# A fourth product by inner products in the first layer of the last sequence, and a new order of that layer

## The chip, the cores and the metric

The kernel runs on one NeuronCore of a Trainium2 chip. The metric is the device time of one execution in microseconds, the median over several runs. TensorE (PE in the rows, its weight loads PEld) multiplies matrices into PSUM, VectorE (DVE), ScalarE (ACT) and GpSimd (POOL) work on elements, and SyncE (SP) issues most of the DMAs. Each engine takes its instructions from a queue of its own; semaphores tie them together.

## The reference

Four sequences of 768 rows go through clustered attention (not touched here) and then through a normalised two-layer network:

```python
mu = np.mean(x, axis=-1, keepdims=True)
var = np.mean((x - mu) ** 2, axis=-1, keepdims=True)
xn = (x - mu) / np.sqrt(var + 1e-06) * g_ln
ch = np.maximum(xn @ w_ch1, 0.0) @ w_ch2     # 768x512 @ 512x2048, then 768x2048 @ 2048x512
return (x + ch)
```

All of it is float32. The change lies in `xn @ w_ch1` of the last sequence.

## The kernel before

Each layer is a matrix product done by Winograd's form of Strassen's method: the operands are cut in two by two blocks, and seven block products with sums before and after them take the place of eight. The block products are numbered 1 to 7 as in the code.

**The outer products.** In the first layer the 2048 columns are 16 chunks of 128; chunks j and j+8 (j = 0 to 7) make one unit. `first_layer(b, j, part)` does outer product `part` of unit j: two chunks of 128 of the inner dimension times 384 columns of x, into one PSUM bank. Products 1, 6, 7 and 4 add up in the same bank `st["x"]`, so each must wait until ScalarE has copied the bank's state so far (`kept`, line 930): after 1 comes p1, after 6 u2, after 7 u3; after 4 the bank is taken out by ScalarE with a ReLU (line 972).

**The inner products.** From sequence 2 on (`paired_layer`), two units (a pair, g = 0 to 3) share some outer products, which are split once more: `inner_products` makes an outer product of a pair out of seven products of one chunk of 128 times 192 columns. The code calls the outer product that is made so by a letter: "A" is product 2, "B" is 5, "C" is 3. The seven inner products come in four steps: step 1 makes inner products 1 and 2, step 2 makes 6 and 5, step 3 makes 7, step 4 makes 4 and 3. Below, "c2" is step 2 of C for the pair before, "A1" step 1 of A for the pair at hand. In each letter the inner products 1, 6, 7 and 4 again add up in one bank: the next of them may start only when the state after the one before has been taken out. For A and C VectorE does that, with an addition (line 1372; in the rows `pi<-x_ps,p` for A and `a<-x_ps,lower` or `pi<-x_ps,lower` for C), for B a copy by ScalarE (line 1374, `kept<-x_ps`). A further VectorE addition (line 1378) finishes each output. PSUM has six banks for the `x` and `z` tiles of all these products.

**Other VectorE work in the layer.** `onto_first(j, l)` (line 1567, 128x768) adds B's result to the u2 and u3 of a pair; C adds onto what it leaves. `outer_sums` (lines 1184, 1186, 1188, 128x768 each) makes the operands of the second layer out of a finished pair. `inner_x` (line 1330, four instructions of 128x192) makes the operands of a letter out of x. `unit_end` takes some jobs of the sequence before from a list (`pending`): an addition (line 1292, `m<-m,rest_x`, 128x768) and a transpose (line 1298, `y<-m`).

**What sets the order.** The order is written out by hand: `OUTER` lists the outer products of a pair slot by slot, and `inner_plan` says which inner steps stand behind each slot. Within a slot an engine's queue gets first the outer product, then what `onto_first` adds, then the inner steps, `inner_x`, the ReLUs (`relu`, line 943), `outer_sums`, the weight loads (`w_load`), and the jobs of `unit_end`. `manual_schedule` keeps this order on TensorE, VectorE, ScalarE and SyncE. The second layer (`deep_layer`, lines 1236 and 1251) follows; its weights come through a ring of ten slots in `w2`, filled by `ring_load`.

The lines that say when a bank may be used again are these, in `inner_products`:

```python
            nc.tensor.matmul(
                bank, p["w"][way], p["x"][way], start=way in (1, 2, 5), stop=True, skip_group_check=True
            )
            if way in add:
                ...
                if p["onto"]:
                    nc.vector.tensor_tensor(o, bank, p["onto"](*at), ALU.add)
                else:
                    nc.scalar.copy(o, bank)
```

Of the kernel before, what the change touches and what calls it, by code (L numbers as in the profile page):

```python
# [23 lines left out]
def kernel(  # L24
# [1297 lines left out]
    w1_d = {n: spill.tile([NPU, P, 4 * P], F32, name=f"w1_d{n}") for n in (2, 5, 3)}  # L1322
# [27 lines left out]
    def w1_pair(j):  # L1350
        return [[w1_block(0, 1, j + i)[:, k] for k in range(2)] for i in range(2)]
# [31 lines left out]
    def flat(t):  # L1383
        return t.rearrange("p a c -> p (a c)")
# [47 lines left out]
    def w_load(b, n, g):  # L1432
# [17 lines left out]
        if b == LAST and n:  # L1450
            nc.sync.dma_start(out=w_in[5][:, 512:] if n == 5 else w_in[n], in_=w1_d[n][g])
# [8 lines left out]
    def inner_plan(g, last):  # L1460

        if not last:
# [17 lines left out]
        plan = {  # L1480
            1: [("C", g - 1, 4), ("B", g, 3)], 2: [("B", g, 4), ("A", g, 1)], 3: [("A", g, 2)],
            4: [("A", g, 3)], 5: [("A", g, 4)], 6: [("C", g, 1)],
            7: [("C", g, 2), ("B", g + 1, 1)], 8: [("C", g, 3), ("B", g + 1, 2)],
        }
        if g == 0:
            plan |= {
                1: [], 2: [("B", g, 1)], 3: [("B", g, 2), ("A", g, 1)], 4: [("A", g, 2), ("B", g, 3)],
                5: [("B", g, 4), ("A", g, 3)], 6: [("A", g, 4), ("C", g, 1)],
            }
        elif g == NPU - 1:  # L1490
            plan |= {5: [("A", g, 4), ("C", g, 1)], 6: [("C", g, 2)], 7: [("C", g, 3)], 8: [("C", g, 4)]}
        return plan

    def paired_layer(b):
# [734 lines left out]
```

## Time and profile before

| | |
|---|---|
| median of 3 runs | 866.61 us (866.16 to 867.55) |
| the profiled execution | 866.26 us, of which the span from first to last instruction is 864.7 us |
| TensorE busy | 859.5 us (99% of the span) |
| VectorE busy | 741.4 us (86%) |
| ScalarE busy | 426.8 us (49%) |
| the chain that ended last | TensorE 97% |
| last sequence's first layer | 729.36 to 796.75 us from the span's start |

The profiled execution lies 0.35 us under the median. Busy time of TensorE is counted from modelled ends, and its instructions overlap, so its spacing is read from the starts.

### The profile page before, as it was taken

Reading aid. Unit: us, or ns where it says so; the run is one execution under the profiler, and the core shown is the slowest. Engines: PE = TensorE matmul, PEld = TensorE weight load, DVE = VectorE, ACT = ScalarE, POOL = GpSimd, SP = SyncE. Lnnn points to the kernel's source line nnn. Section 1 sums busy time; section 2 is a strip of 40 time slices with the busy share of each in tenths; the row PEclk is TensorE's granted clock in tenths of the full one; section 3 lists DMA queues with packets and bytes.
Section 4 is the critical chain, followed back from the end, with each engine's and each line's share of the span. In section 5 each row is a group of like instructions: output and inputs, shape, how many; then the busy total and the mean of one; then the engine's idle time right before and its main releaser. Section 6 shows DMA issues by size and latency. Waiting matters only on the chain.

```text
span 864.7 us, 13888 instructions
## 1 busy us (share of the span) xinstructions
PE 859.5 (99%) x4818; PEld 598.7 (69%) x4818; DVE 741.4 (86%) x1304; ACT 426.8 (49%) x809; POOL 143.5 (17%) x231
## 2 busy tenths in 40 slices
PE   8999999999999999999999999999999999999998
PEld 5444444444444446668887667998778999777998
DVE  6999999999999979888967898898887897776876
ACT  6877789888888836551003543111664110444110
POOL 2012121222222213220000210002440002250000
PEclk9999999999999999999999999999999999999999
DMA  8777889999976538978695688875556975455776
GB/s 165 140 131 132 155 170 188 204 210 207 190 166 179 136 131 234 280 189 313 206 272 151 224 275 247 285 202 176 155 150 207 347 204 178 125 152 171 255 205 139
DMA packets 229354, 169.63 MB, mean 196 GB/s; under 512 B 159056, under 2 KB 180032, under 8 KB 228256
## 3 DMA queue, kind: packets, MB, share of 16 engines
q1 hardware_dynamic: 192768, 139.44, 58.8%
q0 software_dynamic: 11776, 24.79, 13.2%
q10 hardware_dynamic: 24736, 4.48, 2.8%
q8 instruction: 39, 0.64, 0.3%
q14 instruction: 35, 0.29, 0.1%
HBM read 119.67 MB, written 40.59 MB: 185 GB/s over the span
## 4 chain that ended last, share of the span: by engine, by line
PE 97%; DMA 1%; DVE 1%; SPq 0%; ACT 0%; issue 0%; DVEq 0%; ACTq 0%
PE x_ps L901 19%; PE s_ps L426 18%; PE a_ps L438 15%; PE x_ps L1236 12%; PE z_ps L1236 6%; PE x_ps L1018 5%; PE z_ps L901 5%; PE x_ps L1363 5%; PE y_ps L1236 3%; PE z_ps L1018 2%; PE z_ps L1363 2%; PE sim_ps L334 2%; PE den_ps L504 1%; PE y_ps L1018 1%; PE y_ps L1363 1%; DMA out_dram<-y 1%
## 5 line engine op out<-in xcount | busy, mean ns | idle before, releaser
L426 PE MATMUL s_ps<-t,t 64*128 64x384 f32 x768 | 154.7, 483 | 0.0
L1312 POOL DMA_DIRECT2D out_dram<-y x66 | 51.1, 782 | 268.2 <-DVE y L1298 187.9
L426 PEld LDWEIGHTS s_ps<-t,t 64*128 64x128 f32 x768 | 68.0, 187 | 39.1 <-issue 38.1
L1236 PE MATMUL x_ps<-lower,w 128*128 128x192 f32 x448 | 80.5, 326 | 0.0
L1236 PEld LDWEIGHTS x_ps<-lower,w 128*128 128x128 f32 x448 | 74.2, 190 | 0.8
L418 ACT ACTIVATE e<-s_ps 128x768 f32<-128x768 f32 x83 | 66.7, 813 | 3.1 <-PE s_ps L426 2.6
L418 ACT ACTIVATE w<-s_ps 128x768 f32<-128x768 f32 x80 | 64.5, 813 | 4.1 <-PE s_ps L426 3.6
L426 PE MATMUL s_ps<-mask,mask 64*128 64x384 bf16 x384 | 62.7, 323 | 0.3 <-ACT e L418 0.2
L943 ACT ACTIVATE lower<-lower 128x384 f32<-128x384 f32 x88 | 42.9, 520 | 35.5 <-DVE lower L935 30.4
L930 ACT COPY p<-x_ps 128x384 f32<-128x384 f32 x31 | 14.7, 475 | 92.5 <-PE x_ps L901 85.6
L438 PE MATMUL a_ps<-e,v_sb 128*64 128x384 f32 x336 | 57.6, 488 | 0.0
L438 PE MATMUL a_ps<-w,v_sb 128*64 128x384 f32 x320 | 55.2, 488 | 0.0
L303 POOL DMA_DIRECT2D w<-tb x32 | 29.2, 912 | 153.7 <-DVE tb L300 139.9
L901 PE MATMUL x_ps<-xn,w 128*128 128x384 f32 x128 | 46.6, 487 | 0.0
L901 PE MATMUL x_ps<-xn,ws 128*128 128x384 f32 x128 | 46.6, 487 | 0.0
L901 PE MATMUL x_ps<-xt,w 128*128 128x384 f32 x128 | 46.5, 486 | 0.0
L901 PE MATMUL x_ps<-xt,ws 128*128 128x384 f32 x128 | 46.3, 486 | 0.0
L438 PEld LDWEIGHTS a_ps<-e,v_sb 128*64 128x64 f32 x336 | 23.5, 137 | 30.9 <-issue 28.6
L438 PEld LDWEIGHTS a_ps<-w,v_sb 128*64 128x64 f32 x320 | 22.4, 137 | 30.0 <-issue 28.4
L426 PEld LDWEIGHTS <-mask 64*128 64x128 bf16 x384 | 19.0, 94 | 34.3 <-issue 10.4
L1249 ACT COPY u<-x_ps 128x192 f32<-128x192 f32 x30 | 9.6, 319 | 65.9 <-PE x_ps L1236 61.3
L380 ACT ACTIVATE mask<-oh,far 32x384 bf16<-32x384 bf16 x61 | 37.3, 612 | 3.2 <-DVE oh L363 1.9
(347 smaller groups left out, 1894.8 us busy)
## 6 DMA issues: line engine op xcount, KB each, us to landing
w<-w_d SPq DMA_DIRECT2D x84, 256.0 KB, 3.4
raw<-in_moe_w_ch_dram SPq DMA_DIRECT2D x32, 512.0 KB, 4.9
w<-w_t SPq DMA_DIRECT2D x36, 256.0 KB, 5.1
w<-tb POOLq DMA_DIRECT2D x32, 256.0 KB, 5.9
w<-w_all SPq DMA_DIRECT2D x27, 256.0 KB, 3.3
v_sb<-in_v_dram SPq DMA_DIRECT2D x32, 192.0 KB, 3.9
xr<-x_d SPq DMA_DIRECT2D x24, 256.0 KB, 3.5
q_sb<-in_q_dram SPq DMA_DIRECT2D x62, 96.0 KB, 3.9
```

The source lines that it names most:

```text
L303: nc.gpsimd.dma_start(out=w, in_=fb, accum_op=ALU.add)
L334: nc.tensor.matmul(sim[r : r + Q, :HC], cT[:, pr, :, :].rearrange("p j c -> p (j c)"), prepared[n][side][:, g * HC : (g + 1) * HC], start= ...
L380: nc.scalar.activation(out, oh[src, :], AF.Identity, bias=add, scale=factor)
L418: nc.scalar.activation(e, st["both", i][:, :, :HC], AF.Exp, scale=SCALE)
L426: nc.tensor.matmul(banks[j][:, :HC], of_keys[:, keys], of_queries[:, o : o + HC], start=part == first, stop=part != first, skip_group_chec ...
L438: nc.tensor.matmul(acc[j * D : (j + 1) * D, :HC], loaded[n]["v"][:, j, c, :], e[:, j, :], start=(c == 0), stop=(c == NT - 1),)
L901: nc.tensor.matmul(bank[:, :HC], lhs[:, c, :], rhs[:, c], start=first and c == 0, stop=c == NDH - 1, skip_group_check=True,)
L943: nc.scalar.activation(h, h, AF.Relu)
L1018: nc.tensor.matmul(bank[:, :MH].rearrange("p (h f) -> p h f", h=2), hidden[lhs + (c,)][:, tt * P : (tt + 1) * P], rhs[:, :, c], start=firs ...
L1236: nc.tensor.matmul(bank, w[:, c, :], a[:, c], start=(way in (1, 2, 5) or alone) and c == 0, stop=c == NQH - 1, skip_group_check=True,)
L1312: queues[i % len(queues)].dma_start(out=to, in_=y)
L1363: nc.tensor.matmul(bank, p["w"][way], p["x"][way], start=way in (1, 2, 5), stop=True, skip_group_check=True)
```

## The change

Outer product 4 of the last sequence's pairs 0, 1 and 2 is no longer made as two `first_layer(b, j, 4)` per pair, but as a fourth letter, "D", out of seven inner products like the others. Its outcome is added onto u3, which for these pairs is now kept in the place of product 4 (`fourth_inner`). Its x operand is made by `inner_x` in slot 6 of pair 0, its weight sums by `w_sums` during sequence 2 (`FOURTH`: three times four VectorE instructions and a DMA), and they are loaded back pair by pair; room for all this is in slots of the ring in `w2`, so two loads of the ring come later. Pairs 0 to 2 then have six slots instead of eight, `onto_first`, `outer_sums`, `unit_end` and the loads move to other slots, and `inner_plan` has a new list. Lines after 943 move: 1372, 1378, 1330, 1567, 1292 and 1298 are 1377, 1383, 1335, 1604, 1297 and 1303 now, and 1184, 1186, 1188 are 1189, 1191, 1193.

```diff
+    def fourth_inner(b, j):
+        return b == LAST and j < NFH - 2
+
...
-            st["u3"] = kept(st["x"], "u3", hidden_tile(1, NFH + j) if b >= PAIRED else None)
+            st["u3"] = kept(
+                st["x"], "u3", hidden_tile(int(not fourth_inner(b, j)), NFH + j) if b >= PAIRED else None
+            )
...
+        "all": ((0, 1), (1, 1), (0, 6), (1, 6), (0, 7), (1, 7)),
     }
     THIRD = 1
+    FOURTH = ((2, 8), (3, 1), (3, 3))
...
-        if g == 0:
-            plan |= {
-                1: [], 2: [("B", g, 1)], 3: [("B", g, 2), ("A", g, 1)], 4: [("A", g, 2), ("B", g, 3)],
-                5: [("B", g, 4), ("A", g, 3)], 6: [("A", g, 4), ("C", g, 1)],
-            }
...
+        order = (
+            "", "B1", "A1 B2", "A2 B3", "A3 B4", "A4",
+        ) if g == 0 else (
+            "c1 d1", "c2 d2 c3", "d3 c4 B1", "d4 B2 A1", "B3 A2 B4", "A3 C1", "C2 A4 C3", "C4",
+        ) if g == NPU - 1 else (
+            "c1 d1", "c2 d2 c3", "d3 c4 d4", "A1 B1", "A2 B2 A3", "B3 A4 B4",
+        )
...
+            if n == 4:
+                t = w2[:, 7 + g % 2]
+                w_sums(w1_pair(2 * g, 1), parts_of(t, 4))
+                nc.sync.dma_start(out=w1_d[4][g], in_=t)
+                return
...
+        def fourth_of(g):
+            def to(r, h):
+                return hidden_tile(0, NFH + 2 * g + r)[:, half[h]]
+
+            (a11, a12), (_, a22) = w1_pair(2 * g, 1)
+            return {
+                "w": w_operands(a11, a12, a22, parts_of(w_in[4], 4)), "x": x_of[4], "onto": to, "to": to,
+                "keep": keep_in([w_in["parts"][:, i * QC : (i + 1) * QC] for i in range(3)]),
+            }
+
-        makers = {"A": second_of, "B": first_of, "C": third_of}
+        makers = {"A": second_of, "B": first_of, "C": third_of, "D": fourth_of}
...
-            for slot, (r, part) in enumerate(OUTER[inner], 1):
+            short = last and g + 1 < NPU
+            for slot, (r, part) in enumerate(OUTER["all" if short else inner], 1):
...
-                if slot == 7 and (last or g) or slot == 5 and g:
+                if last:
+                    if g and slot == 1:
+                        onto_first(j - 2, 0)
+                        onto_first(j - 2, 1)
+                    if g == NPU - 1 and slot in (6, 7):
+                        onto_first(j, slot - 6)
+                elif g and slot in (5, 7):
                     onto_first(j, slot // 7)
...
-                        onto_first(j, 0)
+                    if slot == 6:
+                        x_of[4] = inner_x(normed[b][3], w_in["x4"])
...
-                sums_at = (2, 3, 4) if last else {THIRD: (3, 4, 7), NPU - 1: (2, 3, 7)}.get(g, (2, 3, 4))
+                sums_at = (5, 6, 7 - short) if last else {THIRD: (3, 4, 7), NPU - 1: (2, 3, 7)}.get(g, (2, 3, 4))
...
-                ends_at = (1, 8) if not last and g == THIRD else (4, 8) if inner else (5, 10)
+                ends_at = (3, 6) if short else (1, 8) if not last and g == THIRD else (4, 8) if inner else (5, 10)
```

How this moves the queues is seen best where one pair ends and the next begins. First TensorE's queue from pair 0 to pair 1, from A's last two products on (a3 are weights of C, w1 of the outer products and of D, line 1368 is line 1363 before). Before:

```order
L1363 MATMUL x_ps_6058<-xi_6045,w1_157 128x192
L1363 MATMUL z_ps_6070<-xn_5624,w_in_5930 128x192
L1363 MATMUL x_ps_6101<-xn_5624,a3_6013 128x192
L1363 MATMUL y_ps_6104<-xn_5624,a3_6013 128x192
L901 MATMUL x_ps_6003<-xt_5983,w1_157 128x384 x2
L1363 MATMUL x_ps_6101<-qs_6027,w_in_5931 128x192
```

and now:

```order
L1368 MATMUL x_ps_6069<-xi_6061,w1_157 128x192
L1368 MATMUL z_ps_6087<-xn_5640,w_in_5946 128x192
L901 MATMUL x_ps_6131<-xn_5640,w1_157 128x384 x2
L1368 MATMUL x_ps_6138<-xn_5640,a3_6029 128x192
L1368 MATMUL y_ps_6141<-xn_5640,a3_6029 128x192
L1368 MATMUL x_ps_6144<-xt_5999,w1_157 128x192
L1368 MATMUL y_ps_6147<-xt_5999,w1_157 128x192
L901 MATMUL x_ps_6158<-xn_5640,w1_157 128x384 x2
L1368 MATMUL x_ps_6138<-qs_6043,w_in_5947 128x192
```

Both blocks end with the first product of step 2 of C; the bank of C is `x_ps_6101` before and `x_ps_6138` now. Between A's end and it stand now two outer products, c1 and d1; before it were c1 and one outer product.

VectorE's queue at the same place, from A's last two additions to the addition that takes c1's bank out. Before:

```order
L1567 TENSOR_TENSOR lower_3190<-qs_6027,lower_3190 128x768
L1372 TENSOR_TENSOR lower_3190<-x_ps_6058,p1_6036 128x192
L1378 TENSOR_TENSOR lower_3190<-z_ps_6070,pi_6032 128x192
L1372 TENSOR_TENSOR a3_6013<-x_ps_6101,lower_3190 128x192
L1378 TENSOR_TENSOR lower_3190<-y_ps_6104,a3_6013 128x192
```

and now:

```order
L1377 TENSOR_TENSOR lower_3190<-x_ps_6069,p1_6052 128x192
L1383 TENSOR_TENSOR lower_3190<-z_ps_6087,pi_6048 128x192
L1335 TENSOR_TENSOR w2_158<-xt_5999 128x192
L1335 TENSOR_TENSOR w2_158<-xt_5999,w2_158 128x192
L1335 TENSOR_TENSOR w2_158<-xt_5999 128x192
L1335 TENSOR_TENSOR w2_158<-xt_5999,w2_158 128x192
L1297 TENSOR_TENSOR m7_5669<-m7_5669,rest_x_5989 128x768
L1303 STREAM_TRANSPOSE y_6121<-m7_5669 128x768
L1604 TENSOR_TENSOR lower_3190<-qs_6043,lower_3190 128x768 x2
L1377 TENSOR_TENSOR a3_6029<-x_ps_6138,lower_3190 128x192
```

Between A's last addition and the taking out of c1's bank there was nothing before; now eight instructions stand there.

The third place is the end of the last pair (g = 3), VectorE again, from the end of B (line 1383 with `kept`) to the addition that takes out the bank of C after the first product of its step 2 (the last row here). Now:

```order
L1383 TENSOR_TENSOR qs_6043<-z_ps_6456,kept_6454 128x192
L1189 TENSOR_TENSOR fifth_3690<-lower_3190 128x768
L1604 TENSOR_TENSOR lower_3190<-qs_6043,lower_3190 128x768
L1377 TENSOR_TENSOR pi_6048<-x_ps_6458,p1_6416 128x192
L1383 TENSOR_TENSOR lower_3190<-z_ps_6480,pi_6048 128x192
L1377 TENSOR_TENSOR a3_6029<-x_ps_6496,lower_3190 128x192
L1383 TENSOR_TENSOR lower_3190<-y_ps_6499,a3_6029 128x192
L1191 TENSOR_TENSOR lower_3190<-lower_3190 128x768
L1211 TENSOR_TENSOR qs_6043<-lower_3190 128x384
L1213 TENSOR_TENSOR lower_3190<-lower_3190 128x12x32
L1604 TENSOR_TENSOR lower_3190<-qs_6043,lower_3190 128x768
L1377 TENSOR_TENSOR a3_6029<-x_ps_6496,lower_3190 128x192
```

Before, the sums of lines 1184 and 1186 and A's additions of its step 3 stood in slots 2 to 4 of this pair, well ahead of this place.

## Rows read from the trace of the kernel before

**Rows 1.** The page: busy time of TensorE, and the chain that ended last.
```profile
PE 859.5 (99%) x4818; PEld 598.7 (69%) x4818; DVE 741.4 (86%) x1304; ACT 426.8 (49%) x809; POOL 143.5 (17%) x231
...
PE 97%; DMA 1%; DVE 1%; SPq 0%; ACT 0%; issue 0%; DVEq 0%; ACTq 0%
```

**Rows 2.** Busy time by stretch: last sequence's first layer; after PE, PEld, DVE, ACT, POOL the granted clock.
```profile
729.36:796.75 67.39, 67.39 (x295) 50.78 (x294) 47.85 (x106) 28.58 (x69) 18.76 (x25) 1.00 0.49 139
```

**Rows 3.** TensorE in order of time in that layer: start, duration, instruction.
```profile
749.52 0.49 PE L1363 MATMUL x_ps<-qs,ws 128*128 128x192 f32 x2
...
750.82 1.45 PE L901 MATMUL x_ps<-xt,ws 128*128 128x384 f32 x4
752.11 0.49 PE L1363 MATMUL x_ps<-xi,w_in 128*128 128x192 f32 x2
...
796.75 1.46 PE L1236 MATMUL x_ps<-lower,w 128*128 128x192 f32 x8
```

**Rows 4.** All engines in order of time, at the layer's one wait of TensorE.
```profile
741.89 0.35 DVE L1372 TENSOR_TENSOR a<-x_ps,lower 128x192 f32<-128x192 f32 x1
742.29 0.30 PEld L1363 LDWEIGHTS x_ps<-qs,w_in 128*128 128x128 f32 x2 [0.44 <-DVE a L1372]
742.30 0.58 PE L1363 MATMUL x_ps<-qs,w_in 128*128 128x192 f32 x2
...
742.72 0.49 PE L1363 MATMUL z_ps<-qs,w_in 128*128 128x192 f32 x2
```

**Rows 5.** VectorE in order of time in that layer.
```profile
739.29 0.35 DVE L1330 TENSOR_TENSOR qs<-xn 128x192 f32<-128x192 f32 x1
...
740.22 0.35 DVE L1330 TENSOR_TENSOR qs<-xn,qs 128x192 f32<-128x192 f32 x1
740.49 0.95 DVE L1567 TENSOR_TENSOR lower<-qs,lower 128x768 f32<-128x768 f32 x1
741.36 0.35 DVE L1372 TENSOR_TENSOR lower<-x_ps,p 128x192 f32<-128x192 f32 x1
...
746.18 0.95 DVE L1292 TENSOR_TENSOR m<-m,rest_x 128x768 f32<-128x768 f32 x1
747.16 0.98 DVE L1298 STREAM_TRANSPOSE y<-m 128x768 f32<-128x768 f32 x1
748.06 0.32 DVE L1372 TENSOR_TENSOR lower<-x_ps,lower 128x192 f32<-128x192 f32 x1
...
752.63 0.36 DVE L1372 TENSOR_TENSOR pi<-x_ps,p 128x192 f32<-128x192 f32 x1 [0.26 <-PE x_ps L1363]
...
754.57 0.36 DVE L1372 TENSOR_TENSOR pi<-x_ps,p 128x192 f32<-128x192 f32 x1 [0.72 <-PE x_ps L1363]
754.97 0.36 DVE L1378 TENSOR_TENSOR lower<-z_ps,pi 128x192 f32<-128x192 f32 x1
```

**Rows 6.** VectorE in order of time, at the end of that layer.
```profile
793.34 0.55 DVE L1206 TENSOR_TENSOR qs<-lower 128x384 f32<-128x384 f32 x1
...
794.40 0.95 DVE L1567 TENSOR_TENSOR lower<-qs,lower 128x768 f32<-128x768 f32 x1
```

**Rows 7.** VectorE in order of time, first layer of sequence 2, where weight sums move in.
```profile
652.17 0.36 DVE L1378 TENSOR_TENSOR qs<-z_ps,kept 128x192 f32<-128x192 f32 x1 [1.23 <-PE z_ps L1363]
...
656.38 0.36 DVE L1372 TENSOR_TENSOR pi<-x_ps,p 128x192 f32<-128x192 f32 x1 [0.72 <-PE x_ps L1363]
...
657.04 0.28 DVE L1341 TENSOR_TENSOR wi<-ws 128x128 f32<-128x128 f32 x1
...
657.97 0.95 DVE L1567 TENSOR_TENSOR lower<-qs,lower 128x768 f32<-128x768 f32 x1
```

**Rows 8.** ScalarE in order of time, an outer copy and an inner one behind it.
```profile
737.65 0.48 ACT L930 COPY lower<-x_ps 128x384 f32<-128x384 f32 x1 [0.97 <-PE x_ps L901]
738.02 0.32 ACT L1374 COPY qs<-x_ps 128x192 f32<-128x192 f32 x1
```

**Rows 9.** DMA issues: count, KB each, median us from issue to landing.
```profile
w_in<-w_d SPq DMA_DIRECT2D x8, 256.0 KB, 2.8
```

More of the change, by code (lines that the diff above doesn't have):

```diff
@@ L1348, in w_operands, with w1_pair @@
         return {1: a11, 2: a12, 3: s4, 4: a22, 5: s1, 6: s2, 7: s3}
[L1350 to L1351 removed]
+    def w1_pair(j, l=0):
+        return [[w1_block(l, 1, j + i)[:, k] for k in range(2)] for i in range(2)]
     half = [slice(h * QC, (h + 1) * QC) for h in range(2)]
@@ L1449, in w_load @@
             nc.sync.dma_start(out=w_in["a3"][:, 2 * P : 3 * P], in_=w1_all[2 * g + 1, :, 896:])
-        if b == LAST and n:
+        elif n in ("s2", "s3"):
+            o = 256 if n == "s2" else 512
+            t, of = w_in[0], w1_all[2 * g : 2 * g + 2]
+            nc.sync.dma_start(
+                out=t.rearrange("p (r c) -> p r c", r=2)[:, :, o - 256 : o],
+                in_=of.rearrange("r p c -> p r c")[:, :, o : o + 256],
+            )
+        if b == LAST and n in w1_d:
             nc.sync.dma_start(out=w_in[5][:, 512:] if n == 5 else w_in[n], in_=w1_d[n][g])
@@ L1479, in inner_plan @@
                 }
[L1480 to L1483, printed above, removed]
[L1484 to L1492 removed]
+        if not last:
+            return {
+                1: [("C", g - 1, 4), ("B", g, 3)], 2: [("B", g, 4), ("A", g, 1)], 3: [("A", g, 2)],
+                4: [("A", g, 3)], 5: [("A", g, 4)], 6: [("C", g, 1)],
+                7: [("C", g, 2), ("B", g + 1, 1)], 8: [("C", g, 3), ("B", g + 1, 2)],
+            }
[5 more added lines that the diff above has]
+            "c1 d1", "c2 d2 c3", "d3 c4 d4", "A1 B1", "A2 B2 A3", "B3 A4 B4",
+        )
+        return {
+            slot: [(w[0].upper(), g - w[0].islower(), int(w[1])) for w in words.split()]
+            for slot, words in enumerate(order, 1)
+        }
     def paired_layer(b):
@@ L1562, in steps @@
             if i == 4 and what != "B":
-                summed.extend(hidden_tile(int(what == "C"), 2 * g + r) for r in range(2))
+                of = {"A": (0, 0), "C": (1, 0), "D": (0, NFH)}[what]
+                summed.extend(hidden_tile(of[0], of[1] + 2 * g + r) for r in range(2))
         def onto_first(j, l):
-            h = place((1, l))[:, j : j + 2].rearrange("p c t -> p (c t)")
-            nc.vector.tensor_tensor(h, fifth_sum, h, ALU.add)
+            h, u = [flat(place((r, l))[:, j : j + 2]) for r in (1, int(not (l and fourth_inner(b, j))))]
+            nc.vector.tensor_tensor(h, fifth_sum, u, ALU.add)
             if l:
@@ L1626, in paired_layer @@
                         inner_keep(5, g + 1)
+                    if (g, slot) in FOURTH:
+                        inner_keep(4, FOURTH.index((g, slot)))
                 relu(summed_first)
-                sums_at = (2, 3, 4) if last else {THIRD: (3, 4, 7), NPU - 1: (2, 3, 7)}.get(g, (2, 3, 4))
+                sums_at = (5, 6, 7 - short) if last else {THIRD: (3, 4, 7), NPU - 1: (2, 3, 7)}.get(g, (2, 3, 4))
                 if g and slot in sums_at:
-                    outer_sums(slice(j - 2, j), True, (sums_at.index(slot),))
+                    outer_sums(slice(j - 2, j), True, [i for i in range(3) if sums_at[i] == slot])
                 if not last and slot in (1, 6) and 0 < j + slot // 6 < NT:
@@ L1638, in paired_layer @@
                         w_load(b, n, g + ahead)
-                ends_at = (1, 8) if not last and g == THIRD else (4, 8) if inner else (5, 10)
+                if short and slot == (5 if g else 3):
+                    w_load(b, 4, g)
+                ends_at = (3, 6) if short else (1, 8) if not last and g == THIRD else (4, 8) if inner else (5, 10)
                 if slot in ends_at:
@@ L1956, in unit_end @@
             if j > 4:
-                for _ in range(4):
+                for _ in range(2 if (b, j) == (LAST, NFH - 2) else 4):
                     if ring["next"] < len(STEPS) * (b - 1) + RING:
```

9 lines of the change are left out of this document (7 added, 2 removed).

## The prediction

> **What bounds the kernel now.** I read the page first: TensorE is busy 99% of the span, and the chain that ended last is 97% TensorE [rows 1]. [...] Then TensorE in order of time. Four inner products start between 749.52 and 750.82, so one costs 0.325 us; an outer product costs 752.11 - 750.82 = 1.29 us [rows 3]. The layer is 31 outer (one of unit 0 was made earlier) and 84 inner products: 31 x 1.29 + 84 x 0.325 = 67.29 us, which from 729.36 ends at 796.65. The second layer starts at 796.75 [rows 3]. So the whole layer holds one wait of 0.1 us, and whatever stalls TensorE here lengthens the kernel by as much.
>
> That one wait is the pattern of everything below. C's second step may only start when VectorE has added out c1's bank. That addition starts at 741.89 and takes 0.35; the weights are loaded at 742.29, 0.05 after its end, and the product after the held one starts 0.42 after it in place of 0.325 [rows 4]. So a TensorE that waits gets on 0.05 us after VectorE ends, and loses 0.1 more because its weight load is no longer hidden.
>
> **What the change takes away.** Six outer products: 6 x 1.29 = 7.74 us. It adds 21 inner ones: 21 x 0.325 = 6.83 us. Net gain of TensorE: 0.91 us, a tenth of a percent. About 0.2% (1.7 us) is what a measurement of this kernel can tell from no change, so the gain alone is too small to be seen, and the order decides.
>
> **What it adds to VectorE.** The distance from one start to the next counts, since these instructions overlap [rows 5]: 0.27 us for 128x192 (740.22 to 740.49), 0.40 where the second needs the first (754.57 to 754.97), 0.87 for 128x768 (740.49 to 741.36), 0.98 for line 1292 with the transpose behind it, 0.90 for the transpose, 1.20 for the four of an `inner_x` (739.29 to 740.49). D brings seven instructions per pair, `inner_x` four once: about 21 x 0.3 + 1.2 = 7.5 us. VectorE would be busy some 55 of 66 us. It has the room on average; what counts is where its work lies.
>
> **The seams between pairs.** Let 0 be the start of a new pair's first outer product. TensorE's queue is then: outer 1.29, c1 0.65, d1 0.65, outer 1.29, and at 3.88 c2. VectorE: the last addition of the old pair follows the last product, which started at -0.325, by 0.52 (752.11 to 752.63 [rows 3, 5]), so it starts at 0.20, and the next instruction can start at 0.47. Then comes the work S that the new order puts ahead of c1's addition, then that addition (0.35) and the 0.05 to TensorE. So c2 can start at 0.87 + S, and TensorE stands still for S - 3.01 us, plus 0.1.
>
> - Pair 0 to 1: `inner_x` 1.20, line 1292 0.98, transpose 0.90, twice `onto_first` 1.74. S = 4.82: 1.81 + 0.1 = 1.91 us.
> - Pair 1 to 2: two `outer_sums` 1.74, line 1292 0.98, transpose 0.90, `onto_first` 1.74. S = 5.36: 2.45 us.
> - Pair 2 to 3: `outer_sums` 1.74, `onto_first` 1.74. S = 3.48: 0.57 us.
>
> Together 4.93 us. Behind the held c2 stand c2's second product, d2 and c3, and nothing else in TensorE's queue may pass. VectorE catches up meanwhile, so the next steps of the pair are in time: d4 needs D's state after d3, 0.52 + 0.35 + 0.05 = 0.92 us after d3's start, and comes 0.975 after it.
>
> The addition of line 1292 and the transpose are moved, not new; before, they ran from 746.18 to 748.06 [rows 5] with no bank waited for behind them.
>
> **The last pair.** Here the new order mixes C and D of pair 2 with B and A of pair 3. When B1 comes, two outer products and C and D hold two banks each: all six. B1 gets the bank of C, when c4's first addition has read it. From d3's start: D's addition at 0.52, its second 0.40 later, c4's 0.27 later, 0.35 long, 0.05: 1.59 us. TensorE is there at 3 x 0.325 = 0.975. Stall 0.62 + 0.1 = 0.72 us.
>
> At the end, count from the start of B's last product. VectorE adds it at 0.52; then, by the third place shown in the change: 0.27, `outer_sums` 0.87, `onto_first` 0.87, A's step 3 0.40 + 0.27, C's step 1 0.40 + 0.27, `outer_sums` 0.87, the two 128x384 of lines 1211 and 1213 1.06 (793.34 to 794.40 [rows 6]), `onto_first` 0.87, and C's addition 0.35 + 0.05: 7.07 us. TensorE's way to C3 is 0.325 + 1.29 + 3 x 0.325 + 1.29 + 4 x 0.325 = 5.18. Stall 1.89 + 0.1 = 1.99 us. After it the start of the second layer meets VectorE as far along as before: the last addition of C is followed by the same instructions.
>
> **What costs nothing, and its cover.** B's copies by ScalarE: the inner one starts 0.37 after an outer one [rows 8] and takes 0.32, so with 0.21 ahead and 0.05 behind it is 0.95 us from B3 to B4, which come 0.975 apart; if that slips, 0.1 each at three places. The weight sums in sequence 2: four take 0.93 us (657.04 to 657.97), and VectorE has gaps of 1.23 at two of the three places and of 0.72 at the third [rows 7]; without cover 0.2 to 0.3 us. The loads: 256 KB land in about 2.8 us [rows 9]; D's are issued after d4 of the pair before and wanted at d2, over ten microseconds later, and the weights of B, asked for at a pair's start, are wanted at its fourth slot (third in the last pair), some 8 us on. In SyncE's queue the loads of D stand behind one that waits for an outer product of the same pair, not for a later one. The two ring loads that move come when the second layer still has four slots loaded ahead.
>
> [...]
>
> **Sum.** 4.93 + 0.72 + 1.99 - 0.91 = 6.73 us. The profiled execution took 866.26 us, 0.35 under the median, and becomes 873.0; the median of 866.61 becomes 873.3 us.
>
> **The rivals.**
>
> 1. Only the seams cost, since in the last pair banks are handed out in another order and the vector work there gets ahead. 866.61 + 4.93 - 0.91 = 870.6 us. For it: in the last pair I count on the allocation of banks, which no row shows.
> 2. No stall, and thus no change: 866.61 - 0.91 = 865.7 us. It would need VectorE to have S down to 3.0 us before c1, its 128x768 instructions some 0.5 us apart at the first two seams, or TensorE to run the products behind the held c2 first. Against it: such instructions are 0.87 apart in [rows 5], and in [rows 4] the products behind the held one came after it. The decisive point is S = 3.0. Another road to the same time: TensorE has slack to catch up. PEld is busy 50.78 of 67.39 us, 75% [rows 2]; yet the distances of 1.29 and 0.325 never shrink after the wait at 742.30. [...]
> 3. VectorE is slower than its distances in the sparse rows say, as by full durations of 0.95 and 0.35: 2 us more, 875.3 us. A second form of it: weights or ring loads arrive late. For it: the layer moves D's 256 KB three times out and three times in.
> 4. TensorE's clock falls after stalls of 2 us. Then one pair's slots, 2.9 us each, cost up to as much again: 876 us and more. Against it: the granted clock is 1.00 in this layer, and nothing here shows it lower.
>
> **How the numbers follow.** My forecast, the full sum, 0.62; rival 1 0.14; rival 2 0.11; rival 3 0.08; rival 4 0.03; something that makes it faster by more than the removed work, 0.02. The first and likeliest gives 873.3 us. The range goes from rival 1 with 0.4 us to spare (870.2) to rival 3 with the uncovered sums and copies (0.3 + 0.3: 875.9). Rival 2 and the clock lie outside. Faster by over 0.2% 0.02, within 0.2% 0.11, slower by over 0.2% 0.87.
>
> **What the profile after would show.** Three waits of TensorE's weight loads for VectorE's line 1377 (`a3<-x_ps`), of about 1.8, 2.35 and 0.5 us, one per seam, each at the second outer product's end of pairs 1, 2 and 3; one for line 1377 at B1 of the last pair, 0.6; one at C's step 3 at the very end, 1.9. Busy time of the removed kind: 25 outer products and 105 inner ones. The layer would take 74.1 us in place of 67.39. The prediction is wrong if the first seam shows VectorE at c1's addition less than 4 us after the pair's first outer product started, or if weights (a DMA) and not line 1377 are what TensorE waits for.

## The result and the profile after

The changed kernel takes 875.47 us (median of 5 runs, 875.01 to 876.54), the kernel before 866.48 us in the runs beside them (866.16 to 867.55). The ratio is 1.0104, with a 95% interval of 1.0089 to 1.0118: about 9 us slower. The profiled execution took 875.54 us with a span of 874.0, against 866.26 and 864.7 before.

Where the 9.3 us of the span lie is read from four stretches. The first view is busy time by stretch in the kernel after, with the columns of [rows 2]: the first layer of sequence 2, its second layer, the last sequence's first layer, and the rest.

```profile
596.35:665.26 68.91, 68.40 (x289) 49.81 (x288) 59.13 (x162) 37.84 (x101) 18.56 (x24) 1.00 0.57 171
665.26:730.25 64.99, 64.99 (x398) 64.46 (x397) 56.41 (x88) 7.74 (x24) 6.19 (x8) 1.00 0.80 257
730.25:805.46 75.21, 68.89 (x313) 52.38 (x312) 55.27 (x131) 27.35 (x68) 18.77 (x25) 1.00 0.47 136
805.46:874.00 68.54, 64.96 (x399) 64.26 (x398) 52.63 (x86) 8.65 (x28) 2.11 (x3) 1.00 0.72 197
```

The same stretches of the kernel before, by the starts of the same products:

```profile
596.50:664.37 67.87, 67.87 (x289) 50.03 (x288) 56.52 (x150) 37.84 (x101) 18.56 (x24) 1.00 0.55 163
664.37:729.36 64.99, 64.99 (x398) 64.46 (x397) 56.44 (x88) 7.73 (x24) 6.19 (x8) 1.00 0.80 257
```

So sequence 2's first layer, where D's weight sums went, got 1.04 us longer; its second layer did not change; the layer of [rows 2] took 75.21 us in place of 67.39, 7.82 more; and the rest 68.54 in place of 67.95. That last 0.59 lies behind the last product (it starts at 870.75, 65.29 us after the second layer's first, as before): the last output transfers ended 3.25 us later instead of 2.66, and the spans of the five executions, 873.5 to 875.0, spread by more than that. What lies ahead of 596 was 0.15 shorter. The sum is 1.04 + 7.82 + 0.59 - 0.15 = 9.30.

TensorE in order of time shows six waits of some length in the changed parts, all of them for line 1377, VectorE's first addition out of a bank, and none for a DMA (the last line is the second layer's first product, which does not wait):

```profile
660.96 0.59 PE L1368 MATMUL x_ps<-x,wi 128*128 128x192 f32 x2 [0.51 <-DVE third L1377]
...
746.92 0.59 PE L1368 MATMUL x_ps<-qs,w_in 128*128 128x192 f32 x2 [1.62 <-DVE a L1377]
...
766.62 0.59 PE L1368 MATMUL x_ps<-qs,w_in 128*128 128x192 f32 x2 [2.16 <-DVE a L1377]
...
784.47 0.59 PE L1368 MATMUL x_ps<-qs,w_in 128*128 128x192 f32 x2 [0.31 <-DVE a L1377]
...
789.23 0.59 PE L1368 MATMUL x_ps<-xt,ws 128*128 128x192 f32 x2 [0.45 <-DVE lower L1377]
...
803.09 0.59 PE L1368 MATMUL x_ps<-qs,w_in 128*128 128x192 f32 x2 [1.78 <-DVE a L1377]
...
805.46 1.46 PE L1241 MATMUL x_ps<-lower,w 128*128 128x192 f32 x8
```

The idle time in brackets is counted from the modelled end of the product before (duration 0.49, while the next may start 0.325 after it), so 0.17 has to be added to each. The three seams are thus 1.79, 2.33 and 0.48, B1 is 0.62, C3 is 1.95. The first seam on VectorE, in order of time, shows what c2 waited for:

```profile
741.73 0.35 DVE L1335 TENSOR_TENSOR w<-xt 128x192 f32<-128x192 f32 x1
...
742.92 0.95 DVE L1297 TENSOR_TENSOR m<-m,rest_x 128x768 f32<-128x768 f32 x1
743.91 0.98 DVE L1303 STREAM_TRANSPOSE y<-m 128x768 f32<-128x768 f32 x1
744.81 1.78 DVE L1604 TENSOR_TENSOR lower<-qs,lower 128x768 f32<-128x768 f32 x2
746.51 0.35 DVE L1377 TENSOR_TENSOR a<-x_ps,lower 128x192 f32<-128x192 f32 x1
```

From D's `inner_x` at 741.73 VectorE is never idle, and c1's addition starts 746.51 - 741.73 = 4.78 us later. That is S, predicted as 4.82. The addition ends at 746.86, and c2 starts 0.06 behind it.

### The profile page after: what moved, and what is told of

It is laid out like the page before. It is cut to its first block, busy times and chain, and to the rows that moved or that the text cites. A ratio compares the mean times of both kernels' runs of the same rounds, so it can differ in the third digit from the quotient of the medians.

```text
span 874.0 us, 13998 instructions
## 1 busy us (share of the span) xinstructions
PE 861.3 (99%) x4836; PEld 599.9 (69%) x4836; DVE 751.0 (86%) x1341; ACT 425.9 (49%) x809; POOL 143.5 (16%) x231
## 4 chain that ended last, share of the span: by engine, by line
PE 93%; DVE 4%; DMA 1%; issue 1%; ACT 0%; ACTq 0%; SPq 0%; DVEq 0%
PE s_ps L426 18%; PE x_ps L901 16%; PE a_ps L438 14%; PE x_ps L1241 11%; PE z_ps L1241 6%; PE x_ps L1023 5%; PE z_ps L901 5%; PE x_ps L1368 5%; PE y_ps L1241 3%; PE z_ps L1023 2%; PE z_ps L1368 2%; PE sim_ps L334 2%; PE den_ps L504 1%; PE y_ps L1023 1%; PE y_ps L1368 1%
## 5 line engine op out<-in xcount | busy, mean ns | idle before, releaser
L943 ACT ACTIVATE lower<-lower 128x384 f32<-128x384 f32 x94 | 45.4, 519 | 43.8 <-DVE lower L935 30.5
L901 PE MATMUL x_ps<-xt,w 128*128 128x384 f32 x104 | 37.8, 486 | 0.0
```

Source lines behind the costliest of these rows:

```text
L901: nc.tensor.matmul(bank[:, :HC], lhs[:, c, :], rhs[:, c], start=first and c == 0, stop=c == NDH - 1, skip_group_check=True,)
L943: nc.scalar.activation(h, h, AF.Relu)
```

## The experiments

Because the executions of different kernels differ ahead of the stage in question (the first ten microseconds alone by up to 1.5 us, see the last section), each run is read by stage: how long sequence 2's two layers, the last sequence's first layer, and the rest took in the profiled execution. The ratio is to the kernel before on the same chip.

| kernel | median us (runs) | ratio, 95% interval | sequence 2, first layer | second layer | last sequence, first layer | rest |
|---|---|---|---|---|---|---|
| before | 866.48 (5) | 1 | 67.87 | 64.99 | 67.39 | 67.95 |
| changed | 875.47 (5) | 1.0104 (1.0089 to 1.0118) | 68.91 | 64.99 | 75.21 | 68.54 |
| e1_ends | 872.09 (5) | 1.0066 (1.0052 to 1.0080) | 68.77 | 64.99 | 71.54 | 68.73 |
| e2_push | 883.06 (5) | 1.0174 (1.0153 to 1.0195) | 69.13 | 64.99 | 82.53 | 68.32 |
| e3_queue | 877.38 (4) | 1.0117 (1.0102 to 1.0133) | 68.84 | 64.99 | 76.75 | 68.12 |
| e4_last | 877.47 (4) | 1.0119 (1.0103 to 1.0134) | 69.06 | 65.94 | 74.16 | 69.03 |
| e5_sums2 | 877.57 (4) | 1.0118 (1.0100 to 1.0135) | 68.41 | 66.47 | 76.84 | 68.28 |
| e6_seams | 871.29 (6) | 1.0045 (1.0031 to 1.0060) | 68.75 | 64.99 | 70.08 | 68.37 |
| e7_all | 871.01 (6) | 1.0043 (1.0029 to 1.0056) | 68.66 | 66.22 | 67.96 | 68.35 |
| e8_all | 869.18 (11) | 1.0025 (1.0016 to 1.0034) | 68.08 | 66.31 | 67.83 | 68.32 |
| e9_after2 | 868.69 (11) | 1.0018 (1.0009 to 1.0027) | 68.29 | 64.99 | 67.82 | 68.54 |
| e10_sum7 | 868.17 (11) | 1.0015 (1.0006 to 1.0024) | 68.74 | 64.99 | 67.52 | 68.95 |

### The two jobs of unit_end off the seams

```diff
-ends_at = (3, 6) if short else ...
+ends_at = ((2, 3) if g < 2 else (3, 6)) if short else ...
```

> The two jobs of unit_end (the 128x768 addition with its transpose, 1.88 us in VectorE's queue) leave the seams: in pairs 0 and 1 they stand in slots 2 and 3 instead of 3 and 6. Same instructions on every engine, another place. Theory (what VectorE's queue holds ahead of c1's addition decides; stall = S - 3.01 + 0.1): S falls from 4.82 to 2.94 at the first seam and from 5.36 to 3.48 at the second, so the first wait (1.6 in the trace) vanishes, the second falls from 2.2 to about 0.4, the third stays; 1.91 + 1.88 = 3.8 us less than the changed kernel's 875.5, 871.7 us. Rival, VectorE simply has too much to do in this layer: the sum of its work is the same, so 875.5. Rival, the loads or PSUM banks are late and VectorE's line is only the last of several releasers: 875.5. Rival, the jobs cost as much where they are put: 873 to 875.5, with a new wait for line 1377 in slots 3 or 4.

The layer took 71.54 us, 3.67 less than in the changed kernel, where 3.8 was expected; the median is 872.09. TensorE in order of time has these four waits left in the layer:

```profile
762.91 0.59 PE L1368 MATMUL x_ps<-qs,w_in 128*128 128x192 f32 x2 [0.31 <-DVE a L1377]
780.77 0.59 PE L1368 MATMUL x_ps<-qs,w_in 128*128 128x192 f32 x2 [0.31 <-DVE a L1377]
785.54 0.59 PE L1368 MATMUL x_ps<-xt,ws 128*128 128x192 f32 x2 [0.46 <-DVE lower L1377]
799.40 0.59 PE L1368 MATMUL x_ps<-qs,w_in 128*128 128x192 f32 x2 [1.78 <-DVE a L1377]
```

The first seam's wait is gone and the second's is 0.31, as S = 2.94 and S = 3.48 demand. VectorE does the same instructions (54.79 us busy in the layer, 55.27 in the changed kernel), so it is not short of time as a whole; its order is what counts.

### More work at the seams

```diff
 if slot in ends_at:
     unit_end(b, j + ends_at.index(slot))
+if short and slot == 6:
+    if g:
+        outer_sums(slice(j - 2, j), True, [2])
+    else:
+        inner_x(normed[b][3], w_in["x4"])
```

> The opposite: at each seam VectorE gets some work twice, behind unit_end in slot 6 (pair 0: D's inner_x, four 128x192, 1.20 us; pairs 1 and 2: the last of outer_sums, 128x768, 0.87 us). Theory: every seam already stalls, so TensorE pays all of it, 1.20 + 0.87 + 0.87 = 2.94 us: 878.4 us, with waits of about 2.8, 3.0 and 1.2 in the trace at the three seams. Rival, VectorE's instructions count by their durations (0.95, 0.36): 3.3 us, 878.8. Rival, TensorE has slack (weight loads busy 70% of the layer) and takes part of it back within the pair: less than half of it, under 877. Rival, another resource holds c2: 875.5.

The three waits came out as expected, 2.82, 3.03 and 1.30. But the median was 883.06, not 878.4, and the five runs go from 878.64 (mean granted clock 1.000) to 883.88 (0.994). The profiled execution, at 883.06, shows what else happened. Busy time by stretch (granted clock in the third column from the right), and TensorE in order of time behind the second seam:

```profile
748.52:752.00 3.48, 3.48 (x12) 3.07 (x13) 1.99 (x7) 1.01 (x3) 3.42 (x5) 0.59 0.46 73
...
770.64:774.00 3.36, 3.36 (x10) 3.36 (x11) 1.61 (x5) 1.02 (x3) 3.36 (x5) 0.50 0.38 59
774.00:777.00 3.00, 3.00 (x8) 1.83 (x8) 0.72 (x2) 0.28 (x1) 0.24 (x1) 0.59 0.21 33
777.00:780.00 3.00, 3.00 (x16) 2.28 (x15) 1.77 (x6) 0.43 (x2) 0.00 (x0) 1.00 0.38 109
```

```profile
770.64 1.01 PE L1368 MATMUL x_ps<-qs,w_in 128*128 128x192 f32 x2 [3.03 <-DVE a L1377]
771.44 0.85 PE L1368 MATMUL z_ps<-qs,w_in 128*128 128x192 f32 x2
772.08 0.85 PE L1368 MATMUL x_ps<-w 128*128 128x192 f32 x2
...
774.00 2.68 PE L901 MATMUL x_ps<-xt,ws 128*128 128x384 f32 x4
776.52 0.49 PE L1368 MATMUL x_ps<-w 128*128 128x192 f32 x2
```

Behind the waits of 2.82 and 3.03 us the granted clock is lower: 0.59 over 748.52 to 752.00, 0.50 over 770.64 to 774.00 and 0.59 over 774.00 to 777.00. Behind the second wait inner products are 0.64 apart (771.44 to 772.08) and the outer one takes 2.52, twice their usual distances of 0.325 and 1.29, until about 776.5. The layer is 82.53 us, 7.32 longer than in the changed kernel. From start to start the three waits are 3.05 longer, where the theory had 2.94. The two stretches from a held c2 to the pair's d4 take 5.69 and 6.85 us in place of 4.14 each, so the clock costs 4.26. One execution had a mean granted clock of 1.000: it took 878.64, 3.1 more than the changed kernel's profiled 875.54, which fits the waits alone (that execution has no profile).

This also decides the form of rival 2 in which TensorE takes time back. In the changed kernel the weight loads are busy 52.38 of 75.21 us, 70%; added work came out in full all the same (3.05 us for 2.94). The layer's products come in chains through a bank, and what was lost in one of them stayed lost.

### Sequence 2: the write-outs on another queue

```diff
-nc.sync.dma_start(out=w1_d[4][g], in_=t)
+nc.gpsimd.dma_start(out=w1_d[4][g], in_=t)
```

What this run was about is seen in the changed kernel. VectorE and SyncE (SPq) in order of time there:

```profile
658.22 0.29 DVE L1346 TENSOR_TENSOR wi<-ws 128x128 f32<-128x128 f32 x1 [1.08 <-DMA ws<-w_all]
```

```profile
651.79 0.32 SPq L1541 DMA_DIRECT2D w_d<-w  x1
652.20 0.38 SPq L1445 DMA_DIRECT2D ws<-w_all  x1
```

The write-out of D's second weight sums (line 1541) stands ahead of a weight load (line 1445) and waits for VectorE; before, that load was issued at 650.26.

> Only the three DMAs that write out D's weight sums in sequence 2 go from SyncE's queue to GpSimd's. VectorE's weight sums stay where they are. In the changed kernel VectorE waits 1.08 us for a weight load (ws<-w_all) that is issued at 652.20, behind the DMA of D's sums at 651.79, where it was issued at 650.26 before; and TensorE then waits 0.51 at 660.96. Theory (the place in SyncE's queue costs it): the load is issued 1.5 to 2 us earlier, both waits vanish, 0.6 to 0.9 us less: 874.6 to 874.9. Rival (the four extra additions of 0.93 us per pair on VectorE cost it): the wait for the load goes, but TensorE's wait stays at 0.3 to 0.5: 875.3. Neither changes the last sequence's layer of 75.2 us.

The load came earlier and its wait went. But the layer took 68.84 us, only 0.07 less, since another wait of VectorE had come in, here in order of time:

```profile
657.03 0.29 DVE L1346 TENSOR_TENSOR w<-w 128x128 f32<-128x128 f32 x1 [0.88 <-DMA w_d<-w]
```

D's third sums need the buffer of the first, and its write-out through GpSimd's queue was not through. So neither theory was tested cleanly: the place in the queue had made the load late, but the edit replaced one late transfer by another. The total is higher than the changed kernel's for reasons apart from it: the start of the program took 1.3 us more, and behind the second seam's wait of 2.16 the granted clock fell (0.58 over 767.90 to 772.00), so that the last sequence's layer took 76.75. The one execution of the four with a mean clock of 1.00 took 875.88, near the changed kernel's 875.47.

### The end of the last pair

```diff
-if g == NPU - 1 and slot in (6, 8):
-    inner_sums(deep[b], ORDER[0], cs=slice(slot - 6, slot - 4))
+if g == NPU - 1 and slot == 8:
+    for c in (0, 2):
+        inner_sums(deep[b], ORDER[0], cs=slice(c, c + 2))
```

> In the last pair the first two 128x384 instructions of inner_sums (lines 1211 and 1213, 1.06 us) move from slot 6 to slot 8, behind C4. Theory (VectorE's queue ahead of C's first additions makes C3's wait of 1.78): the wait falls by 1.06 to about 0.7, 874.4 us, unless the second layer, which needs these operands, starts later by as much; then 875.5 with the wait at its first product instead. Rival (A's additions or the banks hold C3): wait unchanged, 875.5.

TensorE in order of time, at C3 and at the start of the second layer:

```profile
804.61 0.59 PE L1368 MATMUL x_ps<-qs,w_in 128*128 128x192 f32 x2 [0.72 <-DVE a L1377]
...
806.97 1.46 PE L1241 MATMUL x_ps<-lower,w 128*128 128x192 f32 x8
...
810.27 1.54 PE L1241 MATMUL x_ps<-lower,w 128*128 128x192 f32 x8 [0.53 <-DVE lower L1218]
```

C3's wait fell from 1.78 to 0.72 and the layer by 1.05 to 74.16: VectorE's queue ahead of C's first additions made that wait. Most of it was given back at 810.27, where the second layer waits for the later operands: 0.7 with the 0.17 of the modelled end. The edit reached sequence 2 too, which runs the same lines, and lengthened its second layer by 0.95, with nothing gained ahead of it; and the program started 1.5 us later, as in e3_queue. So the total is worse.

### Sequence 2: other slots for D's sums

```diff
-FOURTH = ((2, 8), (3, 1), (3, 3))
+FOURTH = ((2, 8), (3, 3), (3, 5))
```

> In sequence 2, D's second and third weight sums move from slots 1 and 3 of the last pair to slots 3 and 5, with their DMAs in SyncE's queue as in the change. So the load ws<-w_all of slot 2 no longer stands behind one of them, and the buffer of the first sums has been written out long before the third needs it, which is where the run with GpSimd's queue stalled (VectorE waited 0.88 us for that DMA). Theory (two waits of VectorE for transfers make TensorE's 0.51 at 660.96 and the small ones beside it): both waits go, 0.6 to 0.9 us less than the changed kernel: 874.6 to 874.9. Rival (four more VectorE instructions, 0.93 us, cost it wherever they stand in this pair): TensorE still waits 0.3 to 0.6 there, 875.3 to 875.5.

The first layer took 68.41 us, 0.50 less, and TensorE's wait of 0.51 for line 1377 (at 660.96 in the changed kernel) is gone. The second took 66.47, 1.48 more. SyncE and VectorE in order of time:

```profile
665.98 0.37 SPq L1541 DMA_DIRECT2D w_d<-w  x1
670.91 0.32 SPq L1177 DMA_DIRECT2D w<-w_t  x1
...
672.70 0.42 SPq L592 DMA_DIRECT2D xn<-xT_d  x1
```

```profile
677.85 0.96 DVE L655 TENSOR_TENSOR xn<-xn,stat_row 128x768 f32<-128x768 f32 x1 [1.63 <-DMA xn<-xT_d]
```

D's sums lie in slots of the ring, and the ring's next load (line 1177) is issued 4.9 us behind the last write-out; the rows of x behind it in the queue (line 592) are issued at 672.70 instead of 668.81, and VectorE waits 1.63 us for them. Again the loss went to another transfer in SyncE's queue. As in e3_queue, the last sequence's layer (76.84) holds a fall of the granted clock behind the wait of 2.16 (0.60 over 767.76 to 772.00).

### All three seams

```diff
-ends_at = (3, 6) if short else ...
+ends_at = ((2, 3) if g < 2 else (3, 6)) if short else ...
-sums_at = (5, 6, 7 - short) if last else ...
+sums_at = ((4, 5, 6) if short else (5, 6, 7)) if last else ...
```

> The seams alone, all three: unit_end in slots 2 and 3 of pairs 0 and 1, and outer_sums of pairs 1 and 2 in slots 4, 5 and 6 instead of 5, 6 and 6. Then S is 2.94 at the first seam and 3.48 - 0.87 = 2.61 at the others: below 3.01, no wait at any seam. Theory: 4.93 us less than the changed kernel, 870.6 us; what is left are B1 (0.46) and C3 (1.78) of the last pair. Rival, the work that leaves the seams makes TensorE wait where it goes: over 871.5, with waits in slots 3 to 6. Rival, VectorE is too full as a whole: 872 (as with unit_end alone) or more.

TensorE in order of time has two waits left in the layer:

```profile
785.70 0.59 PE L1368 MATMUL x_ps<-xt,ws 128*128 128x192 f32 x2 [0.46 <-DVE lower L1377]
...
799.56 0.59 PE L1368 MATMUL x_ps<-qs,w_in 128*128 128x192 f32 x2 [1.78 <-DVE a L1377]
```

No seam stalls, and the layer took 70.08 us, 5.13 less than in the changed kernel; expected were 4.93. The median is 871.29 for an expected 870.6. The seams were the largest part of the loss, and they were a matter of where a few VectorE instructions stand.

### Everything mended

```diff
-"c1 d1", "c2 d2 c3", "d3 c4 B1", "d4 B2 A1", "B3 A2 B4", "A3 C1", "C2 A4 C3", "C4",
+"c1 d1", "c2 d2 c3 d3", "c4 d4 B1", "B2 A1 B3", "A2 B4", "A3 C1", "C2 A4 C3", "C4",
...
-"c1 d1", "c2 d2 c3", "d3 c4 d4", "A1 B1", "A2 B2 A3", "B3 A4 B4",
+"c1 d1", "c2 d2 c3 d3", "c4 d4", "B1 A1", "B2 A2 B3", "A3 B4 A4",
```

and with it the edits of e5_sums2 and e6_seams, `outer_sums` in slots 4, 5 and 6 of the last pair too, `onto_first` in slot 6, and the first half of `inner_sums` in slot 7 of the last sequence only. In e8_all the pairs between have another order:

```diff
+"c1 d1", "c2 d2 c3 d3", "c4", "", "B1 A1 B2 d4 A2 B3 A3", "B4 A4",
```

> All mended: the seams and sequence 2 as in the two runs beside this one; in the last pair d3 moves ahead of c4 and d4 ahead of B1, B4 comes a slot earlier, both onto_first stand in slot 6, outer_sums in slots 4 to 6, and the first half of inner_sums in slot 7; in the pairs between, d3 goes to slot 2 and B3 to slot 5. The computation is unchanged. Theory (nothing but VectorE's place in the queue cost the time): no wait of TensorE over 0.1 us is left in the layer, which takes about 66.7 us instead of 75.2 and 67.39 before; with 0.6 less in sequence 2 that is 875.5 - 8.5 - 0.6 = 866.4 us, and at best 865.7 (0.91 under before). Rival (D's seven more VectorE instructions per pair cannot all be hidden): the waits appear elsewhere in the layer, or at the second layer's first product as in the run that moved inner_sums (0.5 to 0.8 us): 867 to 869.

> As the run before, but in the pairs between d4, A and B keep only the last two slots, so that no inner product stands right behind the step of its own letter. Theory, second part (products that wait just 0.07 us for their own letter's addition, 16 of them in the changed kernel, make 1.1 us of its layer): 0.2 to 0.3 us less than the run before. Rival (those 0.07 come from something else, for example the distance of a product that starts a bank): the same time.

The layer took 67.96 and 67.83 us, some 1.3 us more than expected and 0.4 to 0.6 more than before. Second-layer waits as in e5_sums2 cost 1.2 to 1.3 more. So the medians, 871.01 and 869.18, miss the expected 866.4. The profiled execution of e7_all, 869.21, is the fastest of its six; the median lies 1.8 us above it, in executions without a profile, so the stages do not explain the difference between the two medians. In the layer one wait of size is left, at C2 of the last pair (0.58 with the 0.17, and 0.1 behind it), and a smaller one at C3 (0.19 and 0.1), here the first, of e8_all, in order of time:

```profile
794.61 0.59 PE L1368 MATMUL x_ps<-qs,w_in 128*128 128x192 f32 x2 [0.42 <-DVE a L1377]
```

The difference between the two orders is 0.13 us in the layer, under the 0.2 to 0.3 expected. Of the 16 small distances of 0.39 to 0.41 in the changed kernel eight are left in e7_all and six in e8_all: two fewer, at 0.07 each, are the 0.13. What makes them is read from the trace, below.

### Sequence 2 once more, and C3

The edits against e8_all:

```diff
-FOURTH = ((2, 8), (3, 3), (3, 5))
+FOURTH = ((2, 8), (3, 2), (3, 3))
...
-if (g, slot) in FOURTH:
+if (g, slot) in FOURTH and slot != 2:
     inner_keep(4, FOURTH.index((g, slot)))
...
 (behind the w_load calls of the slot)
+if not last and (g, slot) == FOURTH[1]:
+    inner_keep(4, 1)
```

and, in e10_sum7 alone, the last of `outer_sums` in slot 7 of the last pair.

> As the run before it (all mended, letters of a pair in the last two slots), but D's weight sums in sequence 2 again at other places: the second behind the weight load of slot 2 of the last pair, so that its DMA stands right behind that load in SyncE's queue and not ahead of it, the third in slot 3 as in the change, so that its buffer, which the second layer's ring needs, is written out early (in the two runs with slots 3 and 5 the ring's load was issued only at 670.4 to 670.9, 5 us behind the DMA of D's sums, and with it the rows of x that VectorE then waited 1.5 us for). Theory (the places in SyncE's queue cost sequence 2 its time): neither the wait for ws<-w_all nor the one for the rows of x over 1 us is left, TensorE's waits at 660 and at 685 go, and the last sequence's layer starts 0.6 us or more earlier than in the run before (730.75): about 866.6 to 867.9 us. Rival (four more VectorE instructions per pair cost it wherever they stand): the layer starts as late, 868.4 to 869.2.

> As the run beside it, and the last of the three outer_sums of the last pair moves from slot 6 to slot 7, out of the way of C's first additions. Theory: C3's wait (0.42 and two small ones, 0.8 in all) goes; but VectorE's end comes 0.87 later, and the second layer waits for it at its first products as in the run that moved inner_sums, 0.3 to 0.6 us. Net 0.2 to 0.5 less than the run beside it. Rival (the second layer has 0.9 us to spare): 0.8 less.

In both, sequence 2's second layer is back at 64.99 us, as the places in SyncE's queue demanded. Its first layer took 68.29 in one and 68.74 in the other, which are the same instructions up to there: 0.42 and 0.87 over before, against 1.04 in the change. Set beside before product by product, both lose the same 0.42 in the last pair, where the changed kernel loses 1.00; VectorE no longer waits for a transfer there. The other 0.45 of e10_sum7 were lost ahead of the first of D's sums (at 648.33), at two weight loads of TensorE, here in order of time:

```profile
612.72 0.30 PEld L1368 LDWEIGHTS x_ps<-xt,ws 128*128 128x128 f32 x2 [0.62 <-DMA ws<-w_all]
...
635.71 0.94 PEld L901 LDWEIGHTS x_ps<-xt,ws 128*128 128x128 f32 x4 [0.26 <-DMA ws<-w_all]
```

So part of the cost is mended and 0.42 stays. Losses of 0.16 to 0.45 us ahead of D's sums stand in six of the eleven profiled executions of the kernels with D, and not in that of the kernel before; what makes those loads late is not shown. In e10_sum7 the wait at C3 is gone. The one at C2 (0.42 in brackets) stayed; the expectation had taken it for part of C3's. The layer took 67.52. The second layer then waited, as expected:

```profile
800.79 1.38 PE L1241 MATMUL x_ps<-lower,w 128*128 128x192 f32 x7 [0.38 <-DVE lower L1218]
```

By stages, from the layer's start to the end of the program, e10_sum7 took 0.1 us more than e9_after2 (0.30 less in the layer, 0.41 more behind it). So its median, 0.52 lower, has about the expected size, but the stages do not show where from. 868.69 and 868.17 us are 1.0018 and 1.0015 of the kernel before: within the 0.2% that a measurement can hardly tell, and on the slow side. No version here beats the kernel before. The 0.91 us that the removed products give back are spent on the 0.4 to 0.9 in sequence 2, on 1.0 to 1.3 at C2 and at C3 or the second layer's start, and on 0.4 at six products that come just too late.

## Why the prediction was right, and where its sum was short

The forecast of 873.3 us was the full sum, with slower over 0.2% at 0.87; measured are 875.47, inside the range. The mechanism is shown: the seams appear and vanish with VectorE's order (e1_ends, e6_seams) and grow by what is put there (e2_push). Point by point:

- **Net gain of TensorE, 0.91 us.** No run measures it alone. It fits: 25 x 1.29 + 105 x 0.325 = 66.38 us, and the layer of e10_sum7 took 67.52 with 0.68 for C2's wait and 0.42 for six small margins, which leaves 66.42.
- **Seams, 4.93 us.** Measured 1.79 + 2.33 + 0.48 + 0.3 = 4.90, and 5.13 by taking them away. The rule "0.05 behind VectorE's end, and 0.1 for the weight load" [rows 4] held at every wait of the changed kernel, with 0.05 or 0.06.
- **Distances, not durations.** The durations are the same after as before (0.95 for 768 elements, 0.35 or 0.36 for 192); but two 128x768 instructions and the way to the next took 746.51 - 744.81 = 1.70, not 1.9. Rival 3 by durations is out: its 2 us were an estimate, 0.95 against 0.87 and 0.35 against 0.27 [rows 5] summed over the seams and the end. That its 875.3 is nearer to 875.47 than my 873.3 is chance. Its second form, weights that arrive late, is part of what sequence 2 lost.
- **Last pair, 0.72 and 1.99.** Measured 0.62 + 0.1 and 1.95 + 0.1. So banks go as I counted them, by the size of the wait and by what ended it (the `lower` addition before 789.23), and rival 1 is out. That the second layer starts "as far along as before" held too: no wait there in the changed kernel. With VectorE's work moved behind C4 it did not hold (e4_last, e10_sum7).
- **"The weight sums in sequence 2 ... without cover 0.2 to 0.3 us": the step that failed.** They cost 1.04. I priced the VectorE instructions against the gaps of [rows 7], and took D's DMAs as hidden by when D's weights are wanted. But a write-out waits in SyncE's queue for VectorE, and what stands behind it is late: a weight load (1.08 us of VectorE's time), or a buffer (e3_queue), or the ring's load and the rows of x (e5_sums2). I weighed SyncE's queue in the last sequence only. How the 1.04 divide is shown in part. 1.00 of them lie in the last pair, behind the first of D's sums. With the write-outs behind that load 0.42 are left there with no wait of VectorE for a transfer, so the queue explains some 0.6, and the remaining 0.42 point to VectorE's own sums, twice four of them within 2.2 us in those runs. With the second and third sums two slots on (e5_sums2, e7_all, e8_all) the last pair loses 0.2 to 0.6, most of it at its last step. In four profiled executions of kernels with the sums where the change has them (the changed one, e1_ends, e2_push, e6_seams) it is 0.5 to 1.0, so one execution fixes these shares only roughly.
- **"d4 ... 0.92 us after d3's start, and comes 0.975 after it": a margin that was none.** The layer took 75.21 us; products (66.38) and waits with their weight loads (7.17 + 0.5) leave about 1.2 us. It lies in 16 places where the next product comes 0.39 to 0.41 later instead of 0.325. Six are at d2 and c3 behind the seams, four at d4 and six at B4. Here is the first d4; VectorE, weight loads and products in order of time, each from its own view:

```profile
750.61 0.36 DVE L1377 TENSOR_TENSOR w<-x_ps,lower 128x192 f32<-128x192 f32 x1 [0.86 <-PE x_ps L1368]
```

```profile
751.02 0.30 PEld L1368 LDWEIGHTS x_ps<-w,w 128*128 128x128 f32 x2
751.41 0.30 PEld L1368 LDWEIGHTS z_ps<-xt,w 128*128 128x128 f32 x2
```

```profile
751.06 0.56 PE L1368 MATMUL x_ps<-w,w 128*128 128x192 f32 x2
751.45 0.56 PE L1368 MATMUL z_ps<-xt,w 128*128 128x192 f32 x2
751.85 1.13 PE L901 MATMUL x_ps<-xt,ws 128*128 128x384 f32 x3
```

d4's product is in time, 0.97 after d3; but its weight load waits for the addition as well, starts at 751.02 instead of 0.16 ahead of the product as its neighbours' do, and the 0.07 are lost behind it. I had compared the addition's end with the product's start. At B4 it is ScalarE's copy that comes just too late, here both engines in order of time:

```profile
759.22 0.32 ACT L1379 COPY kept<-x_ps 128x192 f32<-128x192 f32 x1
...
759.59 0.30 PEld L1368 LDWEIGHTS x_ps<-qs,ws 128*128 128x128 f32 x2
```

The prediction had named that slip, "0.1 each at three places"; it came, with 0.14 at each, and was not in the sum.

- **Rival 4, the clock.** In the changed kernel the mean granted clock was 1.00 in all five executions, so it is no part of this result. But its waits of 1.6 to 2.2 us came near: e3_queue and e5_sums2 have the same second seam (2.16), and there the granted clock fell to 0.58 and 0.60 behind it, and the layer took 1.5 and 1.6 us more. I gave this 0.03 on the ground that no row before showed it lower; no row before had a wait of that length either. The same fall here would have made it 877, outside my range: that it stayed away was luck.

1.0 for sequence 2, 1.2 for the small margins and 0.6 at the end, of which part is chance, are 2.8. Less the 0.15 ahead and what the two executions lie above or under their medians (0.07 and 0.35), that is the 2.2 us between 873.3 and 875.47.

## What to carry to other kernels

A product that is traded for cheaper ones with more additions between them can cost nothing on average and everything at one place: add up what the adding engine has queued, from the last thing that it must wait for to the addition that frees the bank, and compare that with the work TensorE has until it wants the bank, less the lead of its weight load (0.16 us at d4's neighbours). A write-out that an engine must fill first belongs behind the loads of its queue, not ahead of them (here VectorE waited 1.08 us for such a load); moving it is worth checking against everything that stands behind its new place, buffers included. And where the most that a change can give is 0.1%, half a microsecond at any seam decides the sign.

## What the runs showed that was not expected

- **A wait of TensorE can cost twice.** Behind the waits of 2.82 and 3.03 us in e2_push the granted clock was 0.59 over the next 3.48 us, and 0.50 and 0.59 over the next 3.36 and 3.00, and the two together cost 4.26 us more than the waits. No run here shows what decides whether the clock falls: behind the same wait of 2.16 us the granted clock was 1.00 in the changed kernel, and 0.58 and 0.60 over the next four microseconds in e3_queue and e5_sums2:

```profile
766.62:770.86 4.24, 4.24 (x21) 3.41 (x22) 2.79 (x9) 1.49 (x4) 4.24 (x6) 1.00 0.38 58
```

```profile
767.90:772.00 4.10, 4.10 (x13) 3.68 (x14) 2.31 (x7) 1.01 (x3) 4.10 (x6) 0.58 0.39 62
```

(the first row is busy time by stretch of the changed kernel, the second of e3_queue).

- **The first ten microseconds differ.** Eight products of line 334 took 1.47 us in the changed kernel's profiled execution and 2.12 in that of e3_queue, and the whole program ran 1.3 us later from there on; e4_last and e6_seams show the same. e9_after2 came to the stages as late, but lost its 1.2 us mostly between 461 and 470 us. A total of one execution is therefore no measure of an effect of 1 us; a stage is.
